# Dummy matmuls placed earlier, x of pair 0 scaled by two engines, states kept as diagonal blocks, and decays and loads of pair 3 placed otherwise

## The chip, the core and the metric

The kernel runs on one core of one Trainium2 chip. TensorE (PE in the profile; PEld is its weight load) multiplies matrices, VectorE (DVE), ScalarE (ACT) and GpSimd (POOL) work on tiles elementwise, SyncE (SP) issues DMAs; ACT and POOL issue some as well. Each engine executes its own instructions in program order and waits on semaphores for the others. Results of TensorE land in PSUM, from where ACT or DVE bring them to SBUF.

The metric is the time of one execution on the device, in microseconds; smaller is better.

## The reference

A state-space attention is followed by a gated feed-forward layer. Inputs: x [4, 8, 768, 32], a [4, 8, 768], B and C [4, 8, 768, 16], weights 256 x 1536 (gate, value) and 1536 x 256 (out), all float32. Cut to what is computed:

```python
# attention, per batch and head, in chunks of the sequence
cum = cumsum(log(clip(a)))                       # within the chunk
L = exp(cum[i] - cum[j]) * (i >= j)
y_intra = ((C @ B.T) * L) @ x
y_inter = (C @ state) * exp(cum[i])
state = exp(sum(la)) * state + sum_j B[j] x[j] exp(cum[-1] - cum[j])
y = y_intra + y_inter
# feed-forward on tokens: y as [4*768, 8*32]
out = (maximum(y @ w_gate, 0) * (y @ w_val)) @ w_out
```

## The kernel before

**Tiles.** The 3072 tokens are twelve pairs of two chunks of 128 tokens; a batch has three pairs (PPB = 3, six chunks, NC = 6). A pair is named p, its chunks i = 0, 1. The 8 heads x 16 states are split in two halves t of four heads q, so that one matmul sees 128 rows (4 heads, 2 halves, 16 states). The feed-forward works on blocks b of 512 tokens (two pairs): 12 groups f of 128 hidden columns.

**Attention of a pair.** B and C are loaded (`load_bc`, L82), scaled by decay factors and cast to bf16 (`cast_bc` L273, `scale_bc` L278), transposed by TensorE (`transp` L309, with `bank` buffers of PSUM), and evacuated to BT and CT (`bevac` L322, `cevac` L333). `back` (L358) transposes BT back, `backevac` (L365) brings it to SBUF as the stationary operand of the state. `G` (L374) multiplies BT and CT; `gevac` (L388) applies the causal mask and casts, on three engines: ACT copies a part, on which POOL then runs a mask select (`causal`, L166), and DVE multiplies the rest by the mask (L405, L407). `Dm` (L498) multiplies the result gs with x. The state is summed up in one PSUM tile, A_ps: `astep` (L413) adds one chunk, `sevac` (L423) brings it to SBUF with its off-diagonal blocks set to zero (smask), and `inter` (L484) multiplies it with CT. `yevac` (L512) writes the sum of `Dm` and `inter`, transposed and in bf16, to yT. From pair 3 on, `states` (L437) and `spread` (L457) do the state's part with four matmuls of 32 rows of output for each chunk (tile positions 0, 32, 64, 96), which write only the diagonal blocks, and with a DVE product that spreads them.

**Decays.** `cp` is the running product of a (a scan on DVE, L210), and `pick` a selection matrix. TensorE brings the products to token order: `dec_wide` (L220) and `dec_token` (L231) for one pair, with four fp32 matmuls each (eight instructions in the profile), `dec_all` (L241) for the batches, with three. For pair 0, `dec_wide` gives the factors of C, `dec_token` those of x: x is multiplied by the reciprocal r0 (`to_x`, L292). For pairs 1 to 3 they stand in wfac: ACT copies them, and DVE takes the reciprocal.

**Feed-forward.** `gv` (L526) does a group f for 512 tokens, `gvh_mm`, `gvh_relu`, `gvh_mul` (L540 to L562) do one for the 256 tokens of one pair: u = 0 is the first pair of the block, u = 1 the second. `fout` (L572) multiplies by the output weights. Weights are loaded as bf16 by POOL (`weights`, `weights_out`, L152 and L159), in three parts each.

**Order.** The order of each engine is that of the program, fixed by `in_order` (L15). `keep_warm` (L200) writes dummy matmuls on a zero tile, whose result nobody reads. The opening, L614 to L721, is written out by hand; TensorE's order there is: 9 dummies of 512 columns; `dec_wide` of pair 0; `dec_token` of pair 0; transposes of B, then of C, of pair 0 (C a second time into tp2, L627, so that ACT and DVE evacuate the two halves from different tiles); `dec_wide` of pair 1; 2 dummies of 128 columns; `G(0)`; `back(0)`; 3 dummies; `dec_wide` of pair 2; `astep(0, 0)`; `dec_wide` of pair 3; 1 dummy; `Dm(0)`; `inter(0, 1)`; `astep(0, 1)`; transposes of pair 1; gv of f = 0 for pair 0; `G(1)`; `back(1)`; gv of f = 1, 2, 3; `astep(1, 0)`; `Dm(1)`; `inter(1, 0)`, `inter(1, 1)`; `astep(1, 1)`; `dec_all`; gv of pair 1 (u = 1). After that the loop from L723 on goes block by block; `turn` (L679, the transposes) of pair 2 comes in its first block after f = 5, `turn` of pair 3 within the output matmuls.

**Loads on demand.** `held(p)` (L637) makes the tiles of a pair, writes one element of them on DVE, and issues its loads of C, B (and x) from SP; the element's write ties the loads to DVE's place in its order. `held(2)` follows `gevac(0)` and the load of chunk 1 of x of pair 1, `held(3)` follows `gevac(1)`.

## Time and profile before

| | |
|---|---|
| median of 3 timed runs | 127.56 us |
| lowest, highest | 126.98 us, 129.03 us |
| profiled execution | 126.84 us, of which the span 124.8 us |
| ACT busy, in the first 4 us / 4 to 8 / 8 to 12 / 12 to 16 | 1.49 / 1.91 / 2.11 / 3.02 us |
| DVE busy, in the same | 1.76 / 2.55 / 3.58 / 3.60 us |
| POOL busy, in the same | 2.28 / 3.40 / 3.95 / 3.18 us |
| granted TensorE clock in each of them | 1.00 |
| DMA queue of SP (hardware) | 8.43 MB, 44.4% of 16 engines over the span |
| DMA queue of POOL (software) | 2.56 MB, 17.1% |

How to read it: the time of the profiled execution contains some 2 us beyond the span, which is the stretch from the first to the last instruction that the profiler saw. Lines of the timeline give start, length, engine, source line, operation, output and input tile, shape and count; several like instructions are merged in one line. In square brackets stands how long the engine had been idle before the first of them, and what ended that. Ends of matmuls are modelled: a matmul of 256 columns shows 0.27 us, while a stream of them advances by 0.11 each. "DMA to landing" is the time from the start of the issue to the data's arrival. A source line within a helper (L262 `copy`, L288 `scale_bc`) stands for all that call it.

### The profile page before, as it was taken

Reading aid. Unit: us, or ns where it says so; the run is one execution under the profiler, and the core shown is the slowest. Engines: PE = TensorE matmul, PEld = TensorE weight load, DVE = VectorE, ACT = ScalarE, POOL = GpSimd, SP = SyncE. Lnnn points to the kernel's source line nnn. Section 1 sums busy time; section 2 is a strip of 40 time slices with the busy share of each in tenths; the row PEclk is TensorE's granted clock in tenths of the full one; section 3 lists DMA queues with packets and bytes.
Section 4 is the critical chain, followed back from the end, with each engine's and each line's share of the span. In section 5 each row is a group of like instructions: output and inputs, shape, how many; then the busy total and the mean of one; then the engine's idle time right before and its main releaser. Section 6 shows DMA issues by size and latency. Waiting matters only on the chain.

```text
span 124.8 us, 3396 instructions
## 1 busy us (share of the span) xinstructions
PE 120.0 (96%) x1261; PEld 82.5 (66%) x1268; DVE 92.7 (74%) x223; ACT 79.3 (64%) x177; POOL 43.3 (35%) x80
## 2 busy tenths in 40 slices
PE   5999999999999999999999999999999999999990
PEld 2365664578885477884577875577875677864790
DVE  4678898888889955898865798855888856687510
ACT  4166777734888735787735887645987546886420
POOL 6798939531805062805021703132600033000000
PEclk9999999999999999999999999999999999999999
DMA  2999999995979999389632289912200002200022
GB/s 57 164 160 180 179 203 198 168 135 54 188 69 188 112 108 183 91 86 120 80 55 84 90 79 133 112 24 84 84 5 0 0 0 89 84 0 0 0 89 84
DMA packets 73312, 11.92 MB, mean 95 GB/s; under 512 B 66960, under 2 KB 73296, under 8 KB 73296
## 3 DMA queue, kind: packets, MB, share of 16 engines
q1 hardware_dynamic: 63408, 8.43, 44.4%
q0 software_dynamic: 6336, 2.56, 17.1%
q10 hardware_dynamic: 3552, 0.72, 3.6%
q8 instruction: 10, 0.16, 0.6%
q14 instruction: 6, 0.05, 0.1%
HBM read 11.11 MB, written 3.15 MB: 114 GB/s over the span
## 4 chain that ended last, share of the span: by engine, by line
PE 96%; DVE 1%; issue 1%
PE o L579 25%; PE gv L550 22%; PE val L534 15%; PE gate L531 13%; PE w L203 4%; PE g L382 3%; PE y L505 3%; PE tp L320 2%; PE y L494 2%; PE o L591 1%; PE d L225 1%; PE dall L243 1%; PE A_ps L450 1%; PE A_ps L419 1%; PE bt L363 1%
## 5 line engine op out<-in xcount | busy, mean ns | idle before, releaser
L579 PE MATMUL o<-wo,h 128*128 128x256 bf16 x276 | 33.1, 273 | 0.0
L538 DVE TENSOR_TENSOR h<-r,val 128x512 bf16<-128x512 bf16 x42 | 28.8, 685 | 5.5 <-ACT r L537 3.0
L537 ACT ACTIVATE r<-gate 128x512 bf16<-128x512 f32 x42 | 25.1, 597 | 8.1 <-PE gate L531 7.3
L579 PEld LDWEIGHTS <-h 128*128 128x128 bf16 x276 | 25.9, 98 | 5.4 <-issue 2.1
L560 DVE TENSOR_TENSOR h<-r,gv 128x256 bf16<-128x256 bf16 x60 | 24.8, 421 | 4.3 <-ACT r L557 3.5
L534 PE MATMUL val<-yT,wv 128*128 128x512 bf16 x84 | 25.0, 379 | 0.3
L170 POOL TENSOR_SCALAR_AFFINE_SELECT gs<-gs 128x512 bf16<-128x512 bf16 (+1 forms) x24 | 12.1, 526 | 37.3 <-ACT gs L394 37.3
L557 ACT ACTIVATE r<-gv 128x256 bf16<-128x256 f32 x60 | 22.8, 385 | 3.0 <-PE gv L550 0.8
L531 PE MATMUL gate<-yT,wg 128*128 128x512 bf16 x78 | 23.7, 379 | 0.0
L550 PE MATMUL gv<-yT,wg 128*128 128x256 bf16 x120 | 23.3, 273 | 0.0
L550 PE MATMUL gv<-yT,wv 128*128 128x256 bf16 x120 | 23.0, 273 | 0.0
L405 DVE TENSOR_TENSOR gs<-g,masks 128x512 bf16<-128x512 f32 x24 | 15.4, 684 | 5.0 <-PE g L382 4.5
L288 POOL TENSOR_TENSOR bs<-bcr,fac 128x256 bf16<-128x256 f32 x16 | 9.6, 621 | 16.1 <-DMA bcr<-in_B_dram 12.6
L534 PEld LDWEIGHTS <-wv 128*128 128x128 bf16 x84 | 8.2, 98 | 9.9
L550 PEld LDWEIGHTS <-wv 128*128 128x128 bf16 x120 | 11.7, 98 | 1.9 <-DMA wv<-in_moe_w_val_dram 0.3
L550 PEld LDWEIGHTS <-wg 128*128 128x128 bf16 x120 | 11.2, 98 | 1.9 <-issue 0.2
L394 ACT CAST gs<-g 128x512 bf16<-128x512 f32 x12 | 7.1, 590 | 8.4 <-PE g L382 8.4
L262 ACT CAST yT<-y 128x512 bf16<-128x512 f32 (+1 forms) x14 | 7.1, 527 | 7.7 <-PE y L505 4.1
L531 PEld LDWEIGHTS <-wg 128*128 128x128 bf16 x84 | 7.8, 98 | 6.3
L461 DVE TENSOR_TENSOR Sm<-A_ps,smask 128x256 bf16<-128x256 f32 x15 | 5.8, 418 | 6.3 <-PE A_ps L450 6.3
L608 ACT COPY ob<-o 128x512 f32<-128x512 f32 x10 | 5.9, 585 | 4.7 <-PE o L579 4.7
L344 DVE TENSOR_SCALAR CT<-tp,tmask 128x256 bf16<-128x256 bf16 x23 | 7.0, 343 | 0.3 <-PE tp L629 0.3
(92 smaller groups left out, 106.5 us busy)
## 6 DMA issues: line engine op xcount, KB each, us to landing
xr<-in_x_dram SPq DMA_DIRECT2D x20, 128.0 KB, 3.4
out_dram<-ob SPq DMA_DIRECT2D x10, 256.0 KB, 2.2
bcr<-in_C_dram SPq DMA_DIRECT2D x16, 64.0 KB, 3.1
bcr<-in_B_dram SPq DMA_DIRECT2D x16, 64.0 KB, 3.1
wg<-in_moe_w_gate_dram POOLq DMA_DIRECT2D x3, 256.0 KB, 5.0
wv<-in_moe_w_val_dram POOLq DMA_DIRECT2D x3, 256.0 KB, 6.0
wo<-in_moe_w_out_dram POOLq DMA_DIRECT2D x3, 256.0 KB, 5.2
bcr<-in_B_dram SPq DMA_DIRECT2D x4, 128.0 KB, 6.6
```

Source lines behind the costliest of these rows:

```text
L170: nc.gpsimd.affine_select(out=dst, in_=dst, pattern=pattern, compare_op=ALU.is_ge, fill=0.0, base=0, channel_multiplier=-1)
L262: (eng.copy if eng is nc.scalar else eng.tensor_copy)(out=out, in_=in_)
L288: eng.tensor_tensor(out=dst[:, :, t], in0=src[:, :, t], in1=f[:, :, 4 * t:4 * t + 4].to_broadcast([128, n, 4, N]), op=ALU.mult)
L405: nc.vector.tensor_tensor(out=d[:, q], in0=g[q], in1=m, op=ALU.mult)
L531: nc.tensor.matmul(out=g, lhsT=wg[:, k, fs], rhs=yT[:, k, tk], start=(k == 0), stop=(k == 1))
L534: nc.tensor.matmul(out=v, lhsT=wv[:, k, fs], rhs=yT[:, k, tk], start=(k == 0), stop=(k == 1))
L537: nc.scalar.activation(r, g, AF.Relu)
L538: nc.vector.tensor_tensor(out=fst[b][:, f], in0=r, in1=v, op=ALU.mult)
L550: nc.tensor.matmul(out=gv_[:, j], lhsT=(wg, wv)[j][:, k, fs], rhs=yT[:, k, tk], start=(k == 0 and not (early and j)), stop=(k == 1), skip_ ...
L557: nc.scalar.activation(r[:, 0:256], fst[b, f, u][:, 0], AF.Relu)
L560: nc.vector.tensor_tensor(out=fst[b][:, f, u * 256:(u + 1) * 256], in0=fst.pop((b, f, u, "r"))[:, 0:256], in1=fst.pop((b, f, u))[:, 1], op ...
L579: nc.tensor.matmul(out=o[:, ts % 2], lhsT=fst[b][:, f, ts * 128:(ts + 1) * 128], rhs=wo[:, f], start=(f == 0 and new), stop=(f == NF - 1), ...
```

## The change

- **Dummies.** The zero tile has 128 columns instead of 512, and a dummy of 512 columns reads it four times. The opening has ten dummies instead of nine. Four dummies of 128 columns follow `dec_wide` of pair 0, two the transposes of B of pair 0, four instead of two stand ahead of `G(0)`, and two of 512 instead of three follow `back(0)`, now behind a `dec_wide`.
- **Decays.** `dec_token` of pair 0 comes after the transposes of pair 0 instead of before them. `dec_wide` of pair 1 comes after `back(0)`, into a tile d123 with those of pairs 2 and 3; its copy (ACT) and reciprocal (DVE, now from wfac instead of PSUM) follow `gevac(0)` and the loads of pair 2.
- **x of pair 0.** Chunk 1 is multiplied by r0 on DVE and chunk 0 on POOL, where POOL did both; r0 is made after C of pair 0 is evacuated.
- **States.** `astep` writes the diagonal blocks alone, with four matmuls of 32 output rows and 64 columns each, in place of one of 128 x 256. For chunks 1 to 3 of batch 0, `sevac` copies these blocks (128 x 64) on ACT, where DVE multiplied 128 x 256 by smask; `inter` of pairs 0 and 1 then runs eight matmuls with 32 rows in and 32 rows out instead of two of 128 x 128. For chunk 4 of batch 0 `sevac` spreads on DVE, as `spread` does.
- **Order.** `sevac(0, 0)` moves up to just behind `astep(0, 0)`; `transp(1, 1)` stands ahead of `astep(0, 1)`. The loads of C and B of pair 3 (`held(3)`) go from behind `gevac(1)` to behind `yevac(1)`. f = 3 of pair 0 goes to the same place, and two of the three parts of `dec_all` come before `astep(1, 0)` in its stead.
- The arguments `ts` of `scale_bc` and `cevac` keep their default everywhere, and `new_xb` and `spread_one` only name what stood in place: they add no instruction.

```diff
-    warm = const.tile([128, 512], BF16)
+    warm = const.tile([128, 128], BF16)
...
     def keep_warm(n, cols=512):
         w = mm.tile([128, 512], FP32, tag="y", name="w")
+        k = cols // 128
         for _ in range(n):
-            nc.tensor.matmul(out=w[:, 0:cols], lhsT=warm[:, 0:128], rhs=warm[:, 0:cols],
-                             start=True, stop=True)
-
-    keep_warm(9)
+            nc.tensor.matmul(
+                out=w[:, 0:cols].rearrange("p (k c) -> p k c", k=k), lhsT=warm,
+                rhs=warm.rearrange("p (o c) -> p o c", o=1).to_broadcast([128, k, 128]),
+                start=True, stop=True)
+
+    keep_warm(10)
...
     def astep(p, i):
...
-        nc.tensor.matmul(
-            out=A_ps[0], lhsT=st[p]["B"][i], rhs=st[p]["x"][i],
-            start=(c == 0), stop=(c == NC - 2), skip_group_check=True)
+        xi = st[p]["x"][i].rearrange("s (t q d) -> s q t d", t=2, q=4)
+        for q in range(4):
+            nc.tensor.matmul(
+                out=A_ps[0][32 * q:32 * q + 32, 0, 0:64].rearrange("p (t d) -> p t d", t=2),
+                lhsT=st[p]["B"][i][:, 32 * q:32 * q + 32], rhs=xi[:, q],
+                start=(c == 0), stop=True, tile_position=(0, 32 * q),
+                skip_group_check=True)
+
+    NTILE = 2
 
     def sevac(p, i):
-        if 2 * (p % PPB) + i == NC - 1:
+        c = 2 * p + i + 1
+        if c == NC:
             return
-        S[2 * p + i + 1] = n = att.tile([128, 2, 128], BF16, tag="Sm", name="Sm", bufs=5)
-        nc.vector.tensor_tensor(out=n, in0=A_ps[0], in1=smask, op=ALU.mult)
+        if c < 2 * NTILE:
+            S[c] = n = att.tile([128, 64], BF16, tag="Sd", name="Sd")
+            nc.scalar.copy(out=n, in_=A_ps[0][:, 0, 0:64])
+        else:
+            S[c] = spread_one(0)
...
+    def spread_one(k):
+        n = att.tile([128, 2, 128], BF16, tag="Sm", name="Sm", bufs=5)
+        a = A_ps[0][:, 0, 64 * k:64 * k + 64].rearrange("p (t o d) -> p t o d", t=2, o=1)
+        nc.vector.tensor_tensor(
+            out=n.rearrange("p t (q d) -> p t q d", q=4),
+            in0=a.to_broadcast([128, 2, 4, D]),
+            in1=smask.rearrange("p t (q d) -> p t q d", q=4), op=ALU.mult)
+        return n
...
     def inter(p, i):
...
         for t in range(2):
+            if p < NTILE:
+                new = opening(s, t)
+                for q in range(4):
+                    r = slice(32 * q, 32 * q + 32)
+                    nc.tensor.matmul(
+                        out=s["y"][t][r, i].rearrange("s (r m) -> s r m", r=2),
+                        lhsT=Sm[r, 32 * t:32 * t + 32], rhs=ct(p, i, r, t=t),
+                        start=new, stop=True, tile_position=(32 * q, 32 * q),
+                        skip_group_check=True)
+                continue
...
-    d01 = mm.tile([128, 2, 2, 8], FP32, tag="Aps", name="d01")
-    dec_token(d01[:, 0], 0, True)
     cast_bc(0, nc.scalar, B_)
     scale_bc(0, nc.vector, C_, dw)
-    r0 = const.tile([128, 2, 8], FP32)
-    nc.vector.reciprocal(r0, d01[:, 0])
-    to_x(0, nc.gpsimd, r0.rearrange("s i h -> s (i h)"))
+    keep_warm(4, 128)
     transp(0, 0, True)
     bevac(0, nc.scalar)
+    keep_warm(2, 128)
     transp(0, 1, True)
...
     cevac(0, nc.scalar, nc.vector, again=tp2)
-    dec_wide(d01[:, 1], 1, False)
-    nc.scalar.copy(out=wfac[:, 1, 1], in_=d01[:, 1])
-    nc.vector.reciprocal(wfac[:, 1, 0], d01[:, 1])
+    d0 = mm.tile([128, 2, 8], FP32, tag="Aps", name="d0")
+    dec_token(d0, 0, True)
+    r0 = const.tile([128, 2, 8], FP32)
+    nc.vector.reciprocal(r0, d0)
+    new_xb(0)
+    for i, eng in ((1, nc.vector), (0, nc.gpsimd)):
+        eng.tensor_tensor(
+            out=st[0]["x"][i].rearrange("s (h d) -> s h d", d=D), in0=st[0]["xr"][:, i],
+            in1=r0[:, i].to_broadcast([128, NH, D]), op=ALU.mult)
     new_bs(1)
-    keep_warm(2, 128)
+    keep_warm(4, 128)
...
     held(2, with_x=False)
-    keep_warm(3)
-    d23 = mm.tile([128, 2, 2, 8], FP32, tag="tp", name="d23")
-    dec_wide(d23[:, 0], 2, True)
+    d123 = mm.tile([128, 3, 2, 8], FP32, tag="tp", name="d123")
+    d23 = d123[:, 1:3]
+    dec_wide(d123[:, 0], 1, True)
+    nc.scalar.copy(out=wfac[:, 1, 1], in_=d123[:, 0])
+    nc.vector.reciprocal(wfac[:, 1, 0], wfac[:, 1, 1])
+    keep_warm(2)
+    dec_wide(d23[:, 0], 2, False)
     astep(0, 0)
+    sevac(0, 0)
     dec_wide(d23[:, 1], 3, False)
     nc.scalar.copy(out=wfac[:, 2:4, 1], in_=d23)
     keep_warm(1)
-    sevac(0, 0)
...
     inter(0, 1)
+    transp(1, 1, True)
     astep(0, 1)
-    transp(1, 1, True)
     transp(1, 0, True)
...
-    held(3, with_x=False)
     weights(8, NF)
     weights_out(0, 4)
-    for f in (1, 2, 3):
+    for f in (1, 2):
         gvh_mm(0, f, 0)
         gvh_relu(0, f, 0)
+    dall = mm.tile([128, HC, 2, NB, 8], FP32, tag="tp", name="dall")
+    dec_all(dall, range(2))
     astep(1, 0)
...
     yevac(1, nc.scalar, nc.vector)
-    dall = mm.tile([128, HC, 2, NB, 8], FP32, tag="tp", name="dall")
-    dec_all(dall, range(HC))
+    held(3, with_x=False)
+    gvh_mm(0, 3, 0)
+    gvh_relu(0, 3, 0)
+    dec_all(dall, range(2, HC))
```

More of the change, by code (lines that the diff above doesn't have):

```diff
@@ L131, with new_xb @@
     make_identity(nc, identf)
+    def new_xb(p):
+        xb = att.tile([128, 2 * NH * D], BF16, tag="xb", name="xb", bufs=6)
+        st.setdefault(p, {})["x"] = [xb[:, i * NH * D:(i + 1) * NH * D] for i in range(2)]
     def cast_x(p, chunks=(0, 1)):
@@ L136, in cast_x @@
         if "x" not in st.setdefault(p, {}):
-            xb = att.tile([128, 2 * NH * D], BF16, tag="xb", name="xb", bufs=6)
-            st[p]["x"] = [xb[:, i * NH * D:(i + 1) * NH * D] for i in range(2)]
+            new_xb(p)
         for i in chunks:
@@ L276, in cast_bc, with scale_bc @@
             copy(eng, dst[:, :, t], src[:, :, t])
-    def scale_bc(p, eng, js=slice(0, 2), f=None):
+    def scale_bc(p, eng, js=slice(0, 2), f=None, ts=(0, 1)):
         b, c0, _ = place(p)
@@ L286, in scale_bc @@
         n = f.shape[1]
-        for t in range(2):
+        for t in ts:
             eng.tensor_tensor(
@@ L331, in bevac, with cevac @@
         copy(eng, dst, src)
-    def cevac(p, *engs, again=None):
+    def cevac(p, *engs, again=None, ts=(0, 1)):
         s = st[p]
-        s["CT"] = CT = att.tile([128, 2, 2, 128], BF16, tag="CT", name="CT")
+        if "CT" not in s:
+            s["CT"] = att.tile([128, 2, 2, 128], BF16, tag="CT", name="CT")
+        CT = s["CT"]
         src = s["tp"][1].rearrange("s i m -> s (i m)")
-        for t in range(2):
+        for t in ts:
             dst, eng = CT[:, t].rearrange("s i m -> s (i m)"), engs[t % len(engs)]
@@ L458, in spread @@
         for k in range(1 if 2 * (p % PPB) + 2 == NC else 2):
-            S[2 * p + k + 1] = n = att.tile([128, 2, 128], BF16, tag="Sm", name="Sm", bufs=5)
-            a = A_ps[0][:, 0, 64 * k:64 * k + 64].rearrange("p (t o d) -> p t o d", t=2, o=1)
-            nc.vector.tensor_tensor(
-                out=n.rearrange("p t (q d) -> p t q d", q=4),
-                in0=a.to_broadcast([128, 2, 4, D]),
-                in1=smask.rearrange("p t (q d) -> p t q d", q=4), op=ALU.mult)
+            S[2 * p + k + 1] = spread_one(k)
     def y_bank(s, apart=False):
```

## The prediction

> **What bounds the kernel now.** I read the page first, then the chain of waits, then the timeline of the first 20 us.
>
> ```profile
> span 124.8 us, 3396 instructions
> PE 120.0 (96%) x1261; PEld 82.5 (66%) x1268; DVE 92.7 (74%) x223; ACT 79.3 (64%) x177; POOL 43.3 (35%) x80
> ```
>
> TensorE is busy for 96% of the span. The chain of waits (start, length, what, all in us) stays on it from 1.26 us on, and from 15.54 us it has hardly a gap. So a change pays only if it shortens TensorE's own work or a stand of TensorE in the first 20 us, and only the part that no later stand gives back.
>
> ```profile
> 10.87 0.70 PE gv L550 x4
> ...
> 13.82 0.34 PE y L505 x16
> 14.15 0.47 PE y L494 x4
> 14.62 0.11 PE A_ps L419
> 14.73 0.81 PE dall L243 x6
> 15.54 1.85 PE gv L550 x16
> ...
> 18.69 0.43 PE val L534 x2
> 19.12 0.29 PE tp L320 x4
> ...
> 28.13 0.11 PE A_ps L419
> ...
> 66.67 0.34 PE y L505 x16
> 67.00 0.12 PE A_ps L450 x16
> ```
>
> In the timeline (start, length, engine, line; in brackets the idle time before it and what ended it) two stands of TensorE matter.
>
> ```profile
> 1.26 4.02 PE L203 MATMUL w<-warm 128*128 128x512 bf16 x9 [1.26 <-DVE first L118]
> 5.21 0.33 PEld L225 LDWEIGHTS dw<-pick,cp 64*64 64x64 f32 x8 [0.83 <-DVE pick L215]
> 7.68 1.29 DVE L405 TENSOR_TENSOR gs<-g,masks 128x512 bf16<-128x512 f32 x2 [0.20 <-PE g L382]
> 9.24 0.06 DVE L655 MEMSET xr<- 1x1 f32 x1
> 11.06 0.10 PEld L550 LDWEIGHTS <-wv 128*128 128x128 bf16 x1 [0.31 <-DMA wv<-in_moe_w_val_dram]
> 17.76 1.19 POOL L288 TENSOR_TENSOR bs<-bcr,wfac 128x256 bf16<-128x256 f32 x2 [1.99 <-DMA bcr<-in_B_dram]
> 19.01 0.23 PEld L320 LDWEIGHTS <-bs 128*128 128x128 bf16 x4 [0.38 <-POOL bs L288]
> ```
>
> First, the opening ends at 11.06, where the first wv lands (issued by POOL at 5.76, 5.3 us later), not where yT of pair 0 is ready (10.87). Second, the transposes of pair 2 start at 19.01, just behind POOL's scaling of B and C of pair 2, which starts when B of pair 2 lands: issued by SP at 10.39, landed 7.2 us later at 17.6. The chain gives these transposes 0.29 where four cost 0.22 at other places (39.09): TensorE already stands about 0.07 there.
>
> **The change part by part.** *Dummies.* The fill of warm shrinks from 0.27 us (L116, 128x256) to the 0.11 of L187 (128x64), so dummies start near 1.10. At 0.43 apiece (their weight loads start at 1.66, 2.08, 2.51) nine end at 4.95, ten at 5.38; dw could start at 5.21. So dw comes 0 to 0.17 late, I take 0.1, since the one after the ninth already runs where the matmuls become faster (transposes at 5.89 take 0.11 each). Behind dw, four dummies of 128 columns (0.055 each at the later rate, 0.107 at the first) replace eight decay matmuls of 0.34; the transposes of B wait for ACT's cast (5.84) anyway. The two next lie in the wait for C's scaling (6.16). Four instead of two before G(0) add 0.11, of which about 0.06 was wait. G(0) comes about 0.1 late in all; the bounds are 0 and 0.3.
>
> *x of pair 0.* POOL's 1.05 us (L299, 7.67 to 8.72) becomes one half on POOL and one on DVE. POOL's two mask selects then start at about 8.2 instead of 8.68, and pair 0's gs is ready on POOL 0.5 sooner. But on DVE a reciprocal (0.25) and a 128x256 product (0.41 by L427, 0.70 at the ratio 0.485/0.286 that L288 shows on DVE when POOL runs the same beside it) now stand before the gs multiplies of L405, in place of the reciprocal L633 (0.26). Chunk 1 of x landed at 6.97 (1.77+5.2), so the data isn't late. Queued behind that product are L405, L407, the one-element fills of xr and bcr, and behind those SP's loads of x of pair 1 and C, B of pair 2. With d0 done near 7.07, r0 near 7.38 and the product near 7.8, L405 starts at 7.8 for 7.68: all of that 0.12 late (0 to 0.4). Dm(0) is then limited by L407 (9.42) and by TensorE's own queue, where a dec_wide (0.36) stands for a dummy (0.21): 9.6 to 9.7 for 9.76. What is won there ends in the wait for wv at 11.06, which nothing here moves. If that cover were gone, it would be worth 0.1.
>
> *States as blocks.* A step was one matmul of 0.11; it becomes four of 64 columns. L450, the same shape, runs 16 in 0.12: 0.03 for four. Against that, L505, of 128 columns, takes 0.34 for 16 where twice 0.12 would be 0.24, so some 0.10 may go into coming from whole-array work: 0.03 to 0.13 a step, I take 0.08. The Trainium skill's page TensorEngine Tiling (Array Packing), Key Properties, says that a change of tiling mode drains the array; by it I would add such a 0.10 at each step and each inter, and the gain below would go to 0.05. The L450 row, entered from the same mode without that extra, agrees with it, though it doesn't prove it. Inter becomes eight matmuls of 32x32 by 128 columns for two of 0.11: not seen in this trace; 0.12 (twice L450's rate) to 0.33 (L382: eight of 256 columns), I take 0.17, L505's rate, for 0.22. The evacuations go from DVE (0.41) to ACT (about 0.22, as L716), which has idle time of 0.73 and 0.75 around 9.4 and 10.4; the one of chunk 0 of pair 1 stands behind two relus, for 14.1, about where DVE had it (14.28). For pair 2 the DVE form stays, at the same 0.42.
>
> *Pair 1 and decays.* Dm(1) waits for gs of pair 1 (POOL 13.62, DVE 13.58), which follows G(1). That stays at 11.5: its gv ends at 11.4, and CT comes from DVE at 11.37 as before. Before Dm(1), two thirds of dec_all (0.54) and a step (0.08) follow f=2 (12.56 to 13.00): 13.62, so Dm(1) stays at 13.75 (0.08 later if dec_all's 0.16 wait and a step of 0.13 come). From Dm(1) to the gv of the second half: 0.34 + 0.34 + 0.08 + f=3 0.44 + 0.27 = 1.47 against 1.72 in the chain, so 0.25 sooner (between 0.40 sooner and 0.08 later, all bounds in).
>
> *C, B of pair 3* go to SP about 1.3 us later. They landed at 18.2 and 22.24; POOL then needed 1.2 us and stood until 26.71. At 23.6 they still have 1.8 us of cover; gone beyond that, each late us costs one.
>
> *The sum.* The 0.25 meets the transposes of pair 2. If B of pair 2 lands 7.2 us after an issue that is 0.12 later, they start at 19.13 whatever TensorE did before. The one later step (28.13) gives 0.03 back. 124.8 + 0.12 - 0.03 = 124.9 of span; with the 2.04 outside the span of the profiled execution (126.84) that is 126.9. The three timed runs have a median of 127.56, 0.7 above the profiled one, so the upper part of the range is for what is not the kernel's order.
>
> **The rivals.** *B of pair 2 lands sooner* (126.5). C of pair 3, issued at 13.63, landed only 0.63 after B of pair 2, while B took 3.2 after C of its own pair (14.44 to 17.6): it looks as if C of pair 3 had shared its time. Without it for 1.3 us, B gains up to 0.65; the wait of 0.07 goes, and the 0.25 stays: 126.84 - 0.07 - 0.25 - 0.03 = 126.5. Against it: landings keep the order of issue throughout. The Trainium skill's page DMA: Bandwidth & Descriptors, Queues, rings and completion order, says that each engine takes the descriptors of SP's ring in order; by that rule a load behind B takes nothing from it, and the forecast stands.
>
> *DVE is slow ahead of L405* (127.3). The product takes 0.70 beside POOL's, and the late dummy its whole 0.17: pair 2's loads go out 0.45 late, and so B, POOL's scaling and the transposes: 126.84 + 0.45 - 0.03 = 127.3. It decides once C of pair 2 is issued after 10.0 (9.84 now). Against it: POOL waits for its chunk until 7.54, so that the overlap is short.
>
> *The clock drops once* (128.5). The granted clock is 1.00 in every slice of the opening, yet the dummies run at half the later rate until 5.1. If the new order brought one more such stretch of 3.4 us, it would cost 1.7. The longest stand of TensorE after 5.2 is 0.38, and the change adds no longer one. *The blocks run one after another*: the sixteen of inter in pair 1 at 0.055 take 0.88 for my 0.34, the 1.47 becomes 2.01, 0.29 more than before: 127.1.
>
> **Chances.** Forecast 0.45 (126.7 to 127.1); B sooner 0.26; DVE slow 0.13; blocks in a row 0.05; clock 0.03; 0.08 for what I don't see. All but the last two lie within 0.4 us of the profiled time. The range takes 126.0 (B sooner with the 0.40 and a faster run) to 128.2 (DVE slow at the timed median's 0.7 above the profile). 2% is 2.55 us, about what a measurement of this kernel can tell from no change. No faster case reaches it, since no more than about 0.5 us of removable stand and work is left: 0.03 of the unseen. Slower needs two drops of the clock (0.01) or the other 0.05 of the unseen: 0.06. Within: 0.91.
>
> **What would show it.** Right: first wv weight load still behind its DMA near 11.06; C of pair 2 issued at 9.9 to 10.0; transposes of pair 2 behind POOL, with a longer stand of TensorE (0.2 to 0.4) ahead of them. Wrong: those transposes start before 18.8 (B came sooner), gv of pair 0 starts after 11.3, A_ps steps or inter cost more than their bounds, or TensorE shows a stand longer than 0.5 us anywhere after 5.2.

## The result, and the profile after

| | before | changed |
|---|---|---|
| median over all timed runs (20 each) | 129.77 us | 127.74 us |
| lowest, highest | 126.92, 130.87 us | 127.00, 128.94 us |
| profiled execution, and its span | 126.84 us, 124.8 us | 128.54 us, 126.8 us |

The changed kernel takes 1.0049 [1.0025, 1.0072] times as long: half a per cent more, a small loss, and within the 2% that the prediction called the same. Executions more than 1.5% above the fastest of their kernel, thirteen of the kernel before and one of the changed, are left out of that ratio and of the median spans below, which is why the ratio stands above 1 although the median of the left column is the higher one. The forecast was 126.9 us, a shade below the three runs it started from.

The span grew by more than the time did. Its median is 126.0 us for the changed kernel and 125.0 to 125.2 for the kernel before (in the executions of it that the experiments were measured against): 1.0 us more. About 0.3 of that comes back outside the span, where the changed kernel spends 1.7 to 1.8 us in each execution and the kernel before 2.0 to 2.2. What shortens that stretch no trace shows.

The first lines of the page after:

```profile
span 126.8 us, 3483 instructions
PE 122.1 (96%) x1309; PEld 83.8 (66%) x1309; DVE 91.8 (72%) x221; ACT 80.0 (63%) x180; POOL 43.0 (34%) x80
...
PEclk9998699999999999999999999999999999999999
```

TensorE is still the bound, at 96%, and its busy time has grown by 2.1 us. The third line shows why most of that is no matter of the order: in the fifth of 40 slices the granted clock falls to 0.6. The windows of the same trace place it (the numbers ahead of the last three are busy us of PE, PEld, DVE, ACT, POOL, with instruction counts; then the granted clock, the DMA share, GB/s):

```profile
11.00:11.50 0.50, 0.50 (x16) 0.31 (x9) 0.33 (x1) 0.39 (x1) 0.50 (x2) 0.99 1.90 164
11.50:12.00 0.50, 0.50 (x5) 0.36 (x5) 0.50 (x3) 0.26 (x2) 0.50 (x1) 0.50 1.23 192
12.00:13.00 1.00, 1.00 (x11) 0.28 (x9) 0.11 (x1) 0.63 (x3) 0.17 (x1) 0.50 1.16 135
13.00:14.00 1.00, 1.00 (x10) 0.72 (x7) 0.77 (x2) 0.85 (x4) 0.14 (x1) 0.50 0.99 144
14.00:15.00 1.00, 1.00 (x6) 0.53 (x4) 1.00 (x3) 0.92 (x4) 1.00 (x3) 0.55 1.32 205
```

TensorE ran at half the clock from about 11.5 to 14.9 (0.55 as the mean of the last row is half the clock for 0.9 of it), 3.4 us long, and what lies between gv of pair 0 and the second half of gv took 5.82 us (11.61 to 17.43) for 4.52 in another execution of the same program, 1.3 more. So this trace is read for its order and its waits, and a second trace of the changed kernel, E1, for its times.

The timeline after, at the places of the lines shown of before (start, length, engine, line; in brackets the idle time before it and what ended it):

```profile
5.47 0.33 PEld L231 LDWEIGHTS dw<-pick,cp 64*64 64x64 f32 x8 [0.87 <-DVE pick L221]
...
8.05 1.29 DVE L413 TENSOR_TENSOR gs<-g,masks 128x512 bf16<-128x512 f32 x2
...
8.42 0.38 ACT L268 COPY bx<-bt 128x256 bf16<-128x256 bf16 x1
...
8.68 0.39 ACT L410 CAST gs<-g 128x256 bf16<-128x256 f32 x1
8.95 0.20 ACT L697 COPY wfac<-d 128x16 f32<-128x16 f32 x1
9.20 0.33 PEld L231 LDWEIGHTS d<-pick,cp 64*64 64x64 f32 x8 [0.68 <-ACT wfac L697]
...
10.20 0.51 SPq L86 DMA_DIRECT2D bcr<-in_C_dram  x1
...
10.49 0.41 PE L538 MATMUL y<-gs,xb 128*32 128x128 bf16 x16
...
11.61 0.37 PE L583 MATMUL gv<-yT,wg 128*128 128x256 bf16 x1
11.62 0.10 PEld L583 LDWEIGHTS <-wv 128*128 128x128 bf16 x1
...
17.85 1.20 POOL L294 TENSOR_TENSOR bs<-bcr,wfac 128x256 bf16<-128x256 f32 x2 [0.80 <-DMA bcr<-in_B_dram]
...
20.70 0.42 PEld L326 LDWEIGHTS <-bs 128*128 128x128 bf16 x4
```

Before, the second `dec_wide` of this stretch and Dm(0) stood so:

```profile
8.96 0.33 PEld L225 LDWEIGHTS d<-pick,cp 64*64 64x64 f32 x8 [0.17 <-issue]
...
9.76 0.41 PE L505 MATMUL y<-gs,xb 128*32 128x128 bf16 x16
```

Two things differ from before. First, there is a new stand: at 9.20 TensorE's weight load had been idle for 0.68, released by ACT's copy of decays. The two dummies ahead of it cover part of that: they start at 8.41 and advance by 0.22 each, so that TensorE is without work from about 8.85, some 0.35 us. Dm(0), the line at 10.49, started at 9.76 before. Second, the two waits that bounded the opening are no longer waits: the first wv (11.62) has no bracket, since it landed before TensorE came, and the transposes of pair 2 (20.70) neither, since POOL had its scaling done at 19.05. TensorE is simply later than both.

E1, the same kernel at granted clock 0.996, against before, as starts of TensorE's steps:

| step | before | E1 | lag | lag gained in the step |
|---|---|---|---|---|
| dw | 5.21 | 5.43 | 0.22 | 0.22 |
| G(0) | 7.16 | 7.57 | 0.41 | 0.19 |
| Dm(0) | 9.76 | 10.54 | 0.78 | 0.37 |
| gv of pair 0 | 10.87 | 11.67 | 0.80 | 0.02 |
| G(1) | 11.50 | 12.22 | 0.72 | -0.08 |
| Dm(1) | 13.75 | 14.43 | 0.68 | -0.04 |
| gv, second half | 15.47 | 16.19 | 0.72 | 0.04 |
| transposes of pair 2 | 19.01 | 19.67 | 0.66 | -0.06 |
| first output matmul | 24.54 | 25.19 | 0.65 | -0.01 |
| end of the span | 124.8 | 126.1 | 1.3 | 0.65 |

The whole loss of the opening, 0.8 us, is there when the feed-forward starts; the steps from the wait for wv to the first output matmul give back 0.15 of it. The 0.37 between G(0) and Dm(0) is the stand behind ACT's copy. Behind the first output matmul another 0.65 is lost. The state's step of pair 2 costs 0.13 more than before (E7 below), the state matmul of pair 4, which waits for x, 0.75 (what follows it came at 34.74 before and comes at 36.28, from a lag of 0.79), and 0.24 is given back by the end. Before:

```profile
33.77 0.61 POOL L262 CAST xb<-xr 128x512 bf16<-128x512 f32 x1
34.55 0.26 PE L450 MATMUL A_ps<-xb,bs 128*32 128x64 bf16 x12
```

And in E1:

```profile
35.42 0.61 POOL L268 CAST xb<-xr 128x512 bf16<-128x512 f32 x1 [0.88 <-DMA xr<-in_x_dram]
36.08 0.27 PE L478 MATMUL A_ps<-xb,bs 128*32 128x64 bf16 x12 [0.57 <-POOL xb L268]
```

Before, the cast was done 0.17 ahead of TensorE (33.77 + 0.61 to 34.55): that was the cover.

### The profile page after: what moved, and what is told of

Read it like the earlier page. It is cut to its first block, busy times and chain, and to the rows that moved or that the text cites. A ratio compares the mean times of both kernels' runs of the same rounds, so it can differ in the third digit from the quotient of the medians.

```text
span 126.8 us, 3483 instructions
## 1 busy us (share of the span) xinstructions
PE 122.1 (96%) x1309; PEld 83.8 (66%) x1309; DVE 91.8 (72%) x221; ACT 80.0 (63%) x180; POOL 43.0 (34%) x80
## 4 chain that ended last, share of the span: by engine, by line
PE 92%; DMA 3%; ACT 1%; SPq 0%; issue 0%; DVE 0%
PE o L612 25%; PE gv L583 22%; PE val L567 14%; PE gate L564 14%; PE g L390 3%; DMA bcr<-in_B_dram 3%; PE y L538 3%; PE tp L326 2%; PE y L527 1%; PE o L624 1%; PE dall L249 1%; PE A_ps L478 1%; PE w L207 1%; PE d L231 1%; PE A_ps L430 1%; PE y L518 0%
## 5 line engine op out<-in xcount | busy, mean ns | idle before, releaser
L564 PE MATMUL gate<-yT,wg 128*128 128x512 bf16 x84 | 25.0, 379 | 0.0
L583 PE MATMUL gv<-yT,wg 128*128 128x256 bf16 x120 | 24.1, 280 | 0.0
L583 PE MATMUL gv<-yT,wv 128*128 128x256 bf16 x120 | 23.8, 279 | 0.0
L455 DVE TENSOR_TENSOR Sm<-A_ps,smask 128x256 bf16<-128x256 f32 x17 | 6.6, 418 | 6.3 <-PE A_ps L478 6.3
```

What stands on the lines that cost most here:

```text
L564: nc.tensor.matmul(out=g, lhsT=wg[:, k, fs], rhs=yT[:, k, tk], start=(k == 0), stop=(k == 1))
L583: nc.tensor.matmul(out=gv_[:, j], lhsT=(wg, wv)[j][:, k, fs], rhs=yT[:, k, tk], start=(k == 0 and not (early and j)), stop=(k == 1), skip_ ...
```

## The experiments

Sixteen runs: repeats of both kernels, and edits of the one or the other; lines of code that only make room are left out of the diffs. Where an expectation numbers a theory, the first is that the opening is late because the loads that ACT issues (C of pair 0 and others) go out 0.20 us sooner and hold up that of a, the second that the stretch at half the clock makes the difference, the third that TensorE's own work grew (the blocks of the state above all), the fourth that the shared tile of decays makes TensorE wait, and the fifth that the tenth dummy costs. Ratios are against runs of the kernel before on the same chip.

### E1 and E4, E12: repeats of both kernels

No edit. E1 is the changed kernel, E4 and E12 the kernel before.

> The changed kernel once more, for a second trace. Theory 1 (the fill of one element that ACT's first loads wait behind ends 0.2 us sooner, so ACT's loads go out at 1.06 instead of 1.26 and take DMA share from a_sb and B of pair 0): a_sb lands near 4.0 again (3.6 before), B of pair 0 near 5.7 (5.3 before), and the ratio stays near 1.005. Theory 2 (a stretch at half clock in the opening, 11.5 to 14.7 in the first trace of the changed kernel, makes the difference): the trace shows it again or, if it doesn't, the span is near 125 us. Theory 3 (TensorE's own work grew): a trace at full clock still shows more than 0.3 us more between Dm of pair 1 and the second half's gv than before (1.72).

> The kernel before, unchanged, for the clock of each of its executions and a second trace. All theories: ratio 1.000 with an interval of some 0.1%. Theory 2: its executions within 0.3% of the fastest show a mean granted clock of 0.997 or more, and no stretch at half clock in the trace after 5.5 us. Theory 1: a_sb lands at 3.5 to 3.7 again.

> The kernel before once more, for another trace. All theories: 2.60 from G(0) to Dm(0), 2.25 from G(1) to Dm(1), 1.72 from Dm(1) to the gv of the second half, 0.98 from the output matmuls of 27.09 to those behind the state's step, and no wait for x of pair 4.

E1: median 127.82 us of 12, 1.003 [0.9991, 1.0068]; its trace has the 0.68 behind ACT's copy again and the table above. It has no stretch at half the granted clock, and its span is 126.1 all the same, not near 125: the second theory falls as an account of the median. From Dm(1) to the second half of gv it takes 1.76 for 1.72, far from the 0.3 more of the third. E4: median 127.17 us of 14, 0.9978 [0.9942, 1.0013]: a repeat of the kernel before came out 0.22% below itself, and an interval of these repeats reaches some 0.4% to either side, nearly the size of the loss. E12, a single execution, took 128.5 us: its matmuls ran at half rate until about 9.5, and from G(0) to Dm(0) it took 3.40 for 2.60; the later steps were as before (2.23 from G(1) to Dm(1), 1.72 from there to the second half of gv), and x of pair 4 was not waited for. Differences of a few tenths of a us between single traces are therefore read step by step, never from the span.

### E2, E3: the loads of ACT sooner and later

E2 is the kernel before with the fill that ACT's first instruction waits for ahead of that of warm:

```diff
-    warm = const.tile([128, 512], BF16)
-    nc.vector.memset(warm, 0.0)
     first = const.tile([1, 2], FP32)
     nc.vector.memset(first, 0.0)
+    warm = const.tile([128, 512], BF16)
+    nc.vector.memset(warm, 0.0)
```

E3 is the changed kernel with a fill of 128x512 that nobody reads in between:

```diff
     nc.vector.memset(warm, 0.0)
+    spare = const.tile([128, 512], BF16)
+    nc.vector.memset(spare, 0.0)
     first = const.tile([1, 2], FP32)
```

> The kernel before, with the one-element fill ahead of the big fill of the dummies' tile, so that ACT's loads go out at about 1.0 instead of 1.26 and nothing else moves. Theory 1: a_sb lands 0.3 to 0.4 us later than before (3.6) and B of pair 0 too (5.3); the time rises by 0.2 to 0.5 us, ratio 1.002 to 1.004. Theories 2 and 3: a_sb's landing and the time stay within 0.1 us of before.

> The changed kernel with an unused fill of 128x512 on DVE between the dummies' fill and the one-element fill, so that ACT's loads go out at about 1.26 as before while the dummies may still start near 1.05. Theory 1: a_sb lands near 3.6, dw starts near 5.2, the time falls by 0.3 to 0.5 us against the changed kernel, ratio to before near 1.001. Theories 2 and 3: as the changed kernel, ratio near 1.005.

The first load of ACT went out at 0.96 in E2 and at 1.32 in E3 (1.26 before, 1.06 after). The scan of a started at 3.83 and 3.81, and over all the traces between 3.50 and 4.01 without any tie to those loads (3.50 in E15, 4.01 in the changed kernel, both with loads at 1.06). In E3 dw stayed at 5.43. E3 took 127.68 us, 1.0012 [0.9978, 1.0046]; E2's six runs (127.12 to 130.67) are too scattered for a ratio. The theory falls: the loads move neither the scan nor dw.

### E9, E11: the tenth dummy

E9 is the changed kernel with nine, E11 the kernel before with the small tile and ten.

```diff
-    keep_warm(10)
+    keep_warm(9)
```

> The changed kernel with nine instead of ten dummies at the start. Theory 5 (the tenth dummy, at half rate, holds dw at 5.43 however early pick is: 5.41 to 5.47 in seven traces of the changed kernel and its variants, with pick ready between 4.91 and 5.41): dw starts at 5.1 to 5.25 where a_sb lands by 3.7, G(0) 0.2 to 0.4 sooner, and the fastest executions are 0.2 to 0.4 below those of the changed kernel (126.8 instead of 127.0 to 127.2). If the tenth only covers the wait for pick: dw stays within 0.1 of 5.43 and so does the time. With the dummies ending at 4.9, the clock may rise later in some executions.

> The kernel before with the small tile of dummies and ten of them at the start, and nothing else of the change. Theory 5: dw at 5.4, its fastest executions 0.1 to 0.4 us above those of the kernel before (127.0 to 127.3 instead of 126.9). If the dummies at the start cost nothing: within 0.1 us of the kernel before.

E9: dw at 5.01 for 5.43, but the half rate then lasted until about 6.9, and G(0) came at 7.68, no sooner than E1's 7.57. It took 127.62 us, 1.0034 [1.0002, 1.0066]. E11: 0.9988 [0.9947, 1.0028]. So the dummy has a price at dw and none in the time that these intervals resolve. From dw to G(0) it takes 2.60 to 2.67 in the traces with the half rate beyond 6.8 (E4, E5, E9, E11, E12) and 1.95 to 2.43 in the others, and how long that rate lasts changes from execution to execution.

### E5, E6: the wait for ACT's copy of decays

`dec_wide` of pairs 1, 2 and 3 write three regions of one PSUM tile, d123. ACT reads the first of them before TensorE may write the second, and that read is queued on ACT behind two copies of gs and the one of bx. E5 gives the first region back its old place, ahead of G(0), in a tile with those of x of pair 0:

```diff
-    d0 = mm.tile([128, 2, 8], FP32, tag="Aps", name="d0")
+    d01 = mm.tile([128, 2, 2, 8], FP32, tag="Aps", name="d01")
+    d0 = d01[:, 0]
     dec_token(d0, 0, True)
+    dec_wide(d01[:, 1], 1, False)
+    nc.scalar.copy(out=wfac[:, 1, 1], in_=d01[:, 1])
...
-    keep_warm(4, 128)
+    keep_warm(2, 128)
...
-    dec_wide(d123[:, 0], 1, True)
-    nc.scalar.copy(out=wfac[:, 1, 1], in_=d123[:, 0])
...
-    keep_warm(2)
-    dec_wide(d23[:, 0], 2, False)
+    keep_warm(3)
+    d23 = mm.tile([128, 2, 2, 8], FP32, tag="tp", name="d23")
+    dec_wide(d23[:, 0], 2, True)
```

E6 writes all three regions first and reads them with one copy:

```diff
     dec_wide(d123[:, 0], 1, True)
-    nc.scalar.copy(out=wfac[:, 1, 1], in_=d123[:, 0])
-    nc.vector.reciprocal(wfac[:, 1, 0], wfac[:, 1, 1])
-    keep_warm(2)
     dec_wide(d23[:, 0], 2, False)
+    dec_wide(d23[:, 1], 3, False)
+    nc.scalar.copy(out=wfac[:, 1:4, 1], in_=d123)
+    nc.vector.reciprocal(wfac[:, 1, 0], wfac[:, 1, 1])
     astep(0, 0)
     sevac(0, 0)
-    dec_wide(d23[:, 1], 3, False)
-    nc.scalar.copy(out=wfac[:, 2:4, 1], in_=d23)
-    keep_warm(1)
+    keep_warm(2)
```

> The changed kernel with the decays of pair 1 where they were: dec_wide of pair 1 right behind dec_token, ahead of G(0), in one tile with it, copied by ACT there; pairs 2 and 3 in a tile of their own; dummies 2 and 3 as before. Theory 4 (the decays of pairs 1, 2 and 3 share one PSUM tile, so TensorE's dec_wide of pair 2 waits until ACT has copied pair 1's, which stands behind ACT's mask copies: 0.68 us of idle weight load in three traces of the changed kernel): the wait ahead of dec_wide of pair 2 goes; from G(0) to Dm(0) it takes 2.6 us or less instead of 2.98, gv of pair 0 starts 0.3 to 0.5 us sooner after G(0), the time falls by 0.3 to 0.5 us against the changed kernel. Theory 3 (TensorE's own work grew): G(0) to Dm(0) stays above 2.9 and the time stays.

> The changed kernel with the three dec_wide back to back and one ACT copy of all three behind them, then the state's step and two dummies (three in the changed kernel). Theory 4: no wait between the dec_wide; Dm(0) 2.3 to 2.5 us behind G(0) instead of 2.98, Dm(1) 0.5 to 0.6 sooner, and the time 0.4 to 0.7 us below the changed kernel (127.1 to 127.3 in the middle), ratio to before 0.999 to 1.001. Theory 3: no gain beyond the 0.2 of the dummy left out.

Both take the wait away, and neither gains time. E5: from G(0) to Dm(0) 2.48 for 2.97, but from dw to G(0) 2.60 for 2.14 (half rate until about 7.2, and eight fp32 instructions more ahead of G(0)), so that Dm(0) started at 10.51, where it had been; 128.84 us of 4 runs, 1.0111 [1.0052, 1.017]. E6: from G(0) to Dm(0) 2.21 for 2.97, by the stand and by the dummy that it leaves out (0.22), and Dm(0) at 9.86, right behind DVE's last product for gs (9.81). But it took 127.7 us, 1.0046 [1.0029, 1.0064]. Its timeline shows where the gain went:

```profile
9.39 0.42 DVE L415 TENSOR_TENSOR gs<-g,masks 128x256 bf16<-128x256 f32 x1
...
9.86 0.37 SPq L100 DMA_DIRECT2D xr<-in_x_dram  x1
...
14.00 0.40 ACT L268 CAST xb<-xr 128x256 bf16<-128x256 f32 x1 [0.65 <-DMA xr<-in_x_dram]
...
14.46 0.35 PE L538 MATMUL y<-gs,xb 128*32 128x128 bf16 x12 [0.23 <-ACT xb L268]
...
15.11 0.12 PEld L518 LDWEIGHTS <-Sd 32*32 32x32 bf16 x8 [0.26 <-ACT Sd L444]
```

x of pair 1 is issued behind gs on DVE's order, at 9.86, and lands 4.1 us later; in E1 it took 3.3, and it takes 3.8 to 4.1 in E6, E10 and E13, why is open. Dm(1) comes 0.43 sooner than in E1 and waits for it in its midst, and `inter` then waits for ACT's copy of the state, which is queued behind the cast of x: from Dm(1) to the second half of gv it takes 2.39 for 1.76. Pair 4's state waits 0.50 for x, as in E1.

### E7, E8, E15: states and x of pair 0 put back

E7 is the changed kernel with the state of pairs 0 to 2 summed and used as before:

```diff
-        xi = st[p]["x"][i].rearrange("s (t q d) -> s q t d", t=2, q=4)
-        for q in range(4):
...
+        nc.tensor.matmul(
+            out=A_ps[0], lhsT=st[p]["B"][i], rhs=st[p]["x"][i],
+            start=(c == 0), stop=(c == NC - 2), skip_group_check=True)
...
+        nc.vector.tensor_tensor(out=n, in0=A_ps[0], in1=smask, op=ALU.mult)
...
-            if p < NTILE:
...
-                continue
```

E8 and E15 are one kernel, with x of pair 0 multiplied on POOL alone:

```diff
-    new_xb(0)
-    for i, eng in ((1, nc.vector), (0, nc.gpsimd)):
-        eng.tensor_tensor(
-            out=st[0]["x"][i].rearrange("s (h d) -> s h d", d=D), in0=st[0]["xr"][:, i],
-            in1=r0[:, i].to_broadcast([128, NH, D]), op=ALU.mult)
+    to_x(0, nc.gpsimd, r0.rearrange("s i h -> s (i h)"))
```

> The changed kernel with states, their evacuation and inter of pairs 0 and 1 as before (one matmul of 128x256 a step, two of 128x128 for inter, smask on DVE). As recorded in the prediction, the blocks save 0.1 us between Dm(1) and the gv of the second half. If coming from one tiling of the array to another costs 0.1 each time, as the step behind inter (0.14, against 0.04 where Dm follows it) suggests, they save nothing: then Dm(1) to gv of the second half stays at 1.76 plus or minus 0.1, and the time within 0.2 us of the changed kernel. If the blocks are dearer than the old form (theory 3), the time falls by 0.3 us or more.

> The changed kernel with x of pair 0 multiplied on POOL alone. If TensorE's own queue (the wait in theory 4) sets Dm(0), G(0) to Dm(0) stays at 2.98 or rises by less than 0.1, DVE's gs multiplies start 0.4 us sooner, and so do the loads of pair 2. If x on two engines is what makes Dm(0) possible when it comes, Dm(0) is 0.3 us or more later behind G(0).

> The changed kernel with x of pair 0 on POOL alone, timed. If x on two engines carries the loss (DVE's product stands ahead of the gs multiplies and of the loads tied to DVE's place): middle 127.1 to 127.3. If it costs little: 127.5 to 127.8, as the changed kernel.

E7: 127.42 us, 1.0035 [1.0016, 1.0055]. The price of the blocks can be read from the step of pair 2, which stands alone among output matmuls. Before, one instruction:

```profile
27.09 1.04 PE L579 MATMUL o<-wo,h 128*128 128x256 bf16 x8
27.96 0.27 PE L419 MATMUL A_ps<-xb,bx 128*128 128x256 bf16 x1
28.07 1.48 PE L579 MATMUL o<-wo,h 128*128 128x256 bf16 x12
```

And after, four blocks:

```profile
28.98 1.04 PE L612 MATMUL o<-wo,h 128*128 128x256 bf16 x8
29.95 0.21 PE L430 MATMUL A_ps<-xb,bx 128*32 128x64 bf16 x4
30.09 0.61 PE L612 MATMUL o<-wo,h 128*128 128x256 bf16 x4
```

From the first output matmul to the one behind the step it is 0.98 before and 1.11 after, of which the eight output matmuls are 0.87: 0.11 for one, 0.24 for four blocks. E7 has 0.98 again. Of the 0.24, 0.10 lies ahead of the first block (27.96 - 27.09 = 0.87 against 29.95 - 28.98 = 0.97), and 0.14 between the first block and the output matmul behind (29.95 to 30.09). Where the step is followed by Dm, whose matmuls have the same 128x32 shape, Dm comes 0.04 behind it (14.39 to 14.43 in E1). So the four blocks themselves take about 0.04, and entering from whole-array work and going back to it about 0.10 each. The Trainium skill's page TensorEngine Tiling (Array Packing), Key Properties, says that a change of the tiling mode drains the array; these rows agree with it and give it a size here, about 0.1. From Dm(1) to the second half of gv E7 takes 1.74, so the blocks save nothing there (1.76).

E8: 127.22 us in a single execution, DVE's gs at 7.97; E15: 127.43 us, 1.0025 [1.0002, 1.0047]. From G(0) to Dm(0) both still take 2.97 and 2.98, so DVE's product is not what makes Dm(0) late.

### E10, E13, E14: two and three parts put back

E13 is E6 with E15, E14 is E7 with E15, E10 all three.

> The changed kernel with three parts taken back or mended: one ACT copy behind three dec_wide (theory 4), the states and inter of pairs 0 and 1 as before, and x of pair 0 on POOL alone. Theory 4 with the price of the blocks (0.13 for the lone step of pair 2, and what pair 1 shows): Dm(0) 2.2 to 2.4 behind G(0), DVE's gs multiplies and the loads of pairs 1 and 2 about 0.3 sooner than with x on two engines, no wait for x of pair 1 ahead of Dm(1), the time near 127.0 to 127.2 in the middle, 0.5 to 0.7 below the changed kernel and equal to the kernel before within 0.2%. If x of pair 1 or of pair 4 lands last whatever TensorE does, the middle stays at 127.4 to 127.7.

> The changed kernel with one ACT copy behind three dec_wide, and x of pair 0 on POOL alone; states stay blocks. If copy and x carry the loss: middle 127.1 to 127.3, as with all three parts (127.26). If the states do: 127.5 to 127.7. The lone step of pair 2 still costs 0.13 more than one matmul would.

> The changed kernel with states and inter of pairs 0 and 1 as before, and x of pair 0 on POOL alone; TensorE still waits for ACT's copy of pair 1's decays. If theory 4's wait is a main part: middle 127.3 to 127.6 and G(0) to Dm(0) near 3.0. If states and x carry the loss: 127.1 to 127.3.

| | put back | median | ratio to before | median span | first output matmul | from there to the last store's issue |
|---|---|---|---|---|---|---|
| kernel before | | | | 125.0 us | 24.54 | 97.62 |
| changed kernel (trace E1) | nothing | 127.74 us | 1.0049 [1.0025, 1.0072] | 126.0 us | 25.19 | 98.27 |
| E6 | copy of decays | 127.70 us | 1.0046 [1.0029, 1.0064] | 125.8 us | 25.38 | 98.21 |
| E7 | states | 127.42 us | 1.0035 [1.0016, 1.0055] | 125.6 us | 25.44 | 97.63 |
| E15 | x | 127.43 us | 1.0025 [1.0002, 1.0047] | 125.7 us | 25.01 | 98.22 |
| E13 | copy, x | 127.52 us | 1.0021 [0.9985, 1.0057] | 125.7 us | 24.91 | 98.58 |
| E14 | states, x | 127.48 us | 1.0030 [1.0011, 1.0049] | 125.6 us | 25.32 | 97.63 |
| E10 | copy, states, x | 127.26 us | 0.9993 [0.9965, 1.0020] | 125.5 us | 25.16 | 97.63 |

By its time, only E10's interval lies apart from the first one of the changed kernel, and it takes in the kernel before; the interval of the repeat E1, [0.9991, 1.0068], overlaps with it. But E10 is not the kernel before again. Its median span is still 0.5 longer, which the shorter stretch outside it hides (1.7 to 1.9 us for 2.0 to 2.2), and its trace is as late at the first output matmul as E1's, 0.62 for 0.65. The pairs don't single out a part either: E13's 127.52 lies in the range that its expectation gave to the states (127.5 to 127.7), and E14's 127.48 in the one that its expectation gave to the wait (127.3 to 127.6).

The last two columns part the loss, though each is read from one trace only. Up to the first output matmul every one of these kernels is 0.37 to 0.90 late, whatever was put back. Behind it the three with the old states (E7, E10, E14) take what the kernel before takes, to 0.01, and those with blocks take more: 0.14 where x of pair 4 is there in time (the changed kernel's own trace, E9 and E16, all 97.76), which is the 0.13 of the step of pair 2, and up to 0.96 where it isn't. The kernel before has a longer one as well: in E12 it is 97.98, since the state of pair 3 waits for its x.

The timeline of E10 shows why the parts don't simply add up in the opening:

```profile
9.89 0.42 DVE L435 TENSOR_TENSOR Sm<-A_ps,smask 128x256 bf16<-128x256 f32 x1
...
10.23 0.77 DVE L294 TENSOR_TENSOR bs<-bcr,wfac 128x128 bf16<-128x128 f32 x2
...
11.07 0.28 PE L326 MATMUL tp<-ident,bs 128*128 128x128 bf16 x2 [0.41 <-DVE bs L294]
```

With the old states DVE has the mask product to do again, the scaling of C of pair 1 stands behind it, and the transposes of pair 1 wait 0.41 for that: of the 0.7 that Dm(0) has gained (9.81 for E1's 10.54), 0.26 is left at gv of pair 0 (11.41 for E1's 11.67), and at the first output matmul 0.03.

### E16: x of pair 1 sooner

E13 with the load of x of pair 1 ahead of the mask work on gs:

```diff
-    gevac(0, between=lambda: backevac(0, nc.scalar))
     new_x(1)
     nc.vector.memset(st[1]["xr"][0:1, 1, 0, 0:1], 0.0)
     load_x(1, 1, nc.sync)
+    gevac(0, between=lambda: backevac(0, nc.scalar))
     held(2, with_x=False)
```

> As e13, with the load of chunk 1 of x of pair 1 tied to DVE's place ahead of gevac(0) instead of behind it, so that it goes out near 8.0 instead of 9.8. If that load holds Dm(1): Dm(1) comes 2.2 behind G(1) or less with no wait for ACT's cast of x, gv of the second half 0.3 to 0.6 sooner than in e6 (16.39), middle 126.7 to 127.0, below both kernels. If the load then takes share from the first wv (landing near 11.0): gv of pair 0 waits for wv by as much as 0.6 and nothing is won.

It took 127.3 us, 1.0012 [0.9989, 1.0035], above the 126.7 to 127.0 that was expected; its median span is 125.5. The load went out at 7.49 for 9.70, Dm(1) started at 13.74 and the second half of gv at 15.50, level with before (13.75 and 15.47): all that the change had lost in the opening was won back. Then:

```profile
18.07 0.11 PEld L567 LDWEIGHTS <-wv 128*128 128x128 bf16 x2 [0.72 <-DMA wv<-in_moe_w_val_dram]
18.08 0.60 PE L567 MATMUL val<-yT,wv 128*128 128x512 bf16 x2 [0.44 <-DMA wv<-in_moe_w_val_dram]
18.36 1.20 POOL L294 TENSOR_TENSOR bs<-bcr,wfac 128x256 bf16<-128x256 f32 x2 [2.55 <-DVE h L593]
...
19.61 0.22 PEld L326 LDWEIGHTS <-bs 128*128 128x128 bf16 x4 [0.56 <-POOL bs L294]
```

The wv of groups 4 to 7 lands only at 18.07. B of pair 2, issued at 10.01, lands 8.2 us later at 18.2 (7.2 before, 6.2 in E1), POOL scales the pair behind it, from 18.36, though the line names DVE, and the transposes start at 19.61, 0.06 ahead of E1. Everything gained was given back at the next two transfers.

## Why the prediction was wrong, and where it was right

**The step that failed** is the one for Dm(0): "limited by L407 (9.42) and by TensorE's own queue, where a dec_wide (0.36) stands for a dummy (0.21): 9.6 to 9.7 for 9.76. What is won there ends in the wait for wv at 11.06". Dm(0) started at 10.49 in the changed kernel and at 10.54 in E1, and gv of pair 0 at 11.61 and 11.67, past the 11.3 that the prediction itself named as the sign that it was wrong. The step counted what the moved `dec_wide` costs as work on TensorE and left out that its tile is now shared: the second `dec_wide` must wait for ACT's read of the first, and three ACT instructions, of 0.38 to 0.59, are queued ahead of that read. The weight load is idle for 0.68, of which dummies cover a part; some 0.35 are without work, and the step took 0.37 more than before (2.97 for 2.60). E5 and E6 change the tile or the copy, and the wait is gone in both, with 2.48 and 2.21 from G(0) to Dm(0) for 2.97: that this wait made Dm(0) late is shown. That it carries the loss of time is not: neither E5 nor E6 is faster than the changed kernel. The diff has all of it: one `tile` line, the copy's place, and ACT's order.

**Terms that were mis-sized.** dw was to come 0 to 0.17 late and came 0.20 to 0.26 late in most traces with ten dummies (5.41 to 5.47, against 4.96, 5.14 and 5.32 in E15, E13 and E16), since the tenth dummy ran at the half rate too (in the changed kernel's own trace dw also waited for pick, ready at 5.41), and G(0) "about 0.1 late" came 0.35 (after) and 0.41 (E1) late, beyond its bound of 0.3. G(0) moves little with nine dummies (E9), whose trace was at half rate until 6.9; whether the missing dummy made it so is not shown. The state step was put at 0.08 and is 0.24 when it stands in whole-array work, beyond its bound of 0.13; the prediction said that by the drain rule the gain would go to 0.05, called the rule not proven, and took the smaller price. The stretch from Dm(1) to the second half of gv, forecast at 1.47, 0.25 sooner, measured 1.76 for 1.72. In E1 the terms of its sum are 0.32 (Dm), 0.39 (inter), 0.14 (step), 0.54 (f = 3) and 0.37 (the last third of `dec_all`) for 0.34, 0.34, 0.08, 0.44 and 0.27: most of the gain was lost where f = 3 and `dec_all` meet, 0.10 each, and E7, with the old states, has it too (1.74). The turn of pair 2, at which that gain was to be lost, is no wait any more in E1. The 7.2 us from the issue of B of pair 2 to its landing, on which the 19.13 rests, came from one trace: in the others of the kernel before it is 5.0 to 6.9, in those of the changed order 5.5 to 8.2. And the 2.04 outside the span was carried over as it was; it is 1.7 to 1.8 in the changed kernel.

**The late state of pair 4.** The prediction did not speak of x of pair 4; its cover was 0.17. The wait shows in E1 (0.57), E6 (0.50), E13 (0.89) and others with the blocks, and not in the changed kernel's own profile nor in E9, which have them as well; no trace with the old states has it. The second of its two loads lands 4.1 to 5.1 us after its issue in eight of the ten traces with blocks, and 3.1 to 3.6 after it in the other two and in all eight with the old states. What ties the one to the other stays open.

**What held.** DVE's new work ahead of L405 took what was worked out, a product of 0.42. L405 came at 8.05 (7.68 before; forecast 7.8) and C of pair 2 was issued at 10.20 (forecast 9.9 to 10.0) because G(0)'s lag came on top; that is past the 10.0 at which the prediction would have said that DVE is slow, though DVE was not. The blocks of inter do not run one after another: 16 take 0.39 (14.75 to 15.14 in E1), not 0.88. The later loads of C and B of pair 3 cost nothing that a trace shows. The clock's drop, given 0.03, came in the profiled execution itself and cost 1.3 of the 1.7 worked out for it; that its 128.5 is the profiled 128.54 is luck, since the opening's lag is in the latter too. B of pair 2 landing sooner was not decided: the spread of its landings, above, is as wide without the change.

**The class** was right, within 2%, and the size was not: the sum gave 0.09 us over the profile of before (0.12 - 0.03), and the runs show 0.5%, some 0.6 us. E1's table has about that at the first output matmul (0.65), but only by chance: the span grew by 1.0, and 0.3 came back outside it. The forecast of 126.9 was also set against one profiled execution, 126.84 us, the lowest of the four times at hand then; measured against their median it read as a gain that no step of it contained.

**What is not settled.** That the blocks cost time behind the first output matmul is shown by the traces: 0.13 at the step of pair 2 in each, and the wait for x of pair 4 in most. What keeps the opening 0.4 to 0.9 late with each of the three parts put back, and with all of them, is not shown, beyond the waits named in each trace; the later `dec_token` of pair 0, the dummies behind it and the earlier transposes of pair 1 were put back in no run. Nor is it shown why the stretch outside the span is shorter. No version here beats the kernel before; by their times E10, E13 and E16 cannot be told from it, by their spans they are 0.5 to 0.7 longer.

## What to carry to other kernels

When a change puts several results into one PSUM tile, read who evacuates each of them and what is queued ahead on that engine: here the second write waited for the first read, and matmuls counted at 0.36 brought a stand of about 0.35 with them. An opening that is fed by a row of transfers has a wait behind every wait; before pricing a saved tenth, look for the next landing, ask how much cover it has, and read its spread from more than one trace. Read the span and the time both, since what lies outside the span can move too. And set the forecast against the median of the timed runs, with the profiled execution only as the scale of the steps.

## What the runs showed of the hardware

**The half rate at the start has no fixed length.** The dummies run at 0.43 per 512 columns at first. Full rate came near 5.2 in the profile of before, near 6.9 in E9, 7.2 in E5, 9.5 in E12 and as late as 17 in the traces of E4 and E11 (executions of 130.87 and 130.63 us), all while the profile's granted clock says 1.00. In the changed kernel's profile a second stretch of 3.4 us came at 11.5, and there the granted clock does show 0.50; in the 5 us before it the longest idle time of a weight load was the 0.68 of 9.20, and TensorE's matmuls stood still for about 0.35 of it. The Trainium skill's page TensorE: Matmul & The Clock Gate, What's actually happening, describes a free-running window of about 3.4 us and a start that differs from run to run; the 3.4 us agree with the window, while half rate until 9.5 or 17 is far longer than one.

**A region of a PSUM tile was not free by itself.** The weight load of a matmul into one region of d123 waited 0.68 or 0.69 for ACT's read of another in the changed kernel's two traces and in the six others that keep that order (E3, E7, E8, E9, E14, E15). Whether the chip asks for that wait or only this program does, no run shows.

**Equal loads land at different times.** The second load of x of pair 4, the same bytes at the same place of the order, took 3.1 us (E7) to 5.1 us (E6, E13) from issue to landing, B of pair 2 5.0 (E11) to 8.2 (E16).

**A change of the tiling mode costs about 0.1 us here.** Four 128x32 matmuls of 64 columns between whole-array matmuls took 0.24, where they take 0.04 if work of the same shape follows.
